# Second-half transposes of a fused mixer kernel by 32x32 VectorE blocks and a DRAM round trip instead of TensorE, and one scan fewer per convolution step

## The chip, the core and the metric

The kernel runs on one core of a Trainium2 chip. The metric is the device time of one execution in microseconds (us). The engines that matter are TensorE (PE in the profile; its weight loads are PEld), VectorE (DVE), ScalarE (ACT), GpSimd (POOL) and SyncE (SP), which issues nearly all DMAs. Each engine runs its own instructions in the order in which they were written down for it; semaphores make one engine wait for another.

## The reference, cut to what matters

The input is one sequence of 2048 rows and 448 columns, in fp32.

```
x = A_u                                        # [1, 2048, 448]
g = sigmoid((x * gate_w).sum(-1))
a = causal_convolution(x, K) + x * D_skip      # K[d, l] = 2 Re sum_n C exp(A dt l), 256 states n
h = gelu(layernorm(x) @ w1); hs = shift(h) @ w2; x1 = x + hs
b = x1 + gelu(layernorm(x1) @ w3) @ w4         # w3 448 -> 1792, w4 1792 -> 448
out = g * a + (1 - g) * b
```

For the inputs here the states decay slowly, and the kernel computes the convolution as a cubic Taylor sum: per column four running sums over time with the coefficients nu[0..3], nested into each other (a flag checks that this holds; otherwise a general path follows, which does not run here).

## The kernel before

The rows are cut into NB = 4 blocks b of 512 rows, each of NT = 4 tiles i of 128 rows. The work on TensorE is a list of 72 **units**: 16 of kind "a" (the w1/w2 mixer, 4 per block), then 56 of kind "d" (the w3/w4 MLP, 14 per block: units 16 to 29, 30 to 43, 44 to 57, 58 to 71). Every fp32 product is made of three products of split high and low halves. A unit n of kind "d" is `first(n)`, 11 matmuls (line 378) into a PSUM tile `p1` (two buffers), then gelu on ACT (line 396, out to `uf`), a copy to the high half `uh` (line 402), the low half `ul` by DVE (line 406, called `act_tail`), and `second(n)`, 12 matmuls (line 433) into four PSUM accumulators. PE does `first` two units ahead (LAG = 2). After the last unit of a block, DVE adds the four accumulators to `xs` (line 442).

From unit OWN = 28 on, the order on each engine is the order in which the code is written (`manual_schedule`, lines 764 to 779); before that a scheduler orders the instructions. For each unit, in this order: `act_tail(n+1)`, the lists `before` and `after` of that unit, `first(n+2)` with its gelu, the list `between`, the copy, some convolution work (`ssm_some`), the list `late`, `second(n)`.

Two other streams are laid into the units:

- **The layer norm of the MLP input**, for block b at units s0 = 9, 20, 30, 45. `norm` (lines 317 to 324) normalises one tile of 128 rows on ACT into `xn`; `norm_t` transposes it on PE, four matmuls 128x128 against the identity `idt` (line 334) into a PSUM tile `misc`, and ACT copies the high half to `xh` (line 336); `norm_lo` makes the low half on DVE (lines 343 and 344). `weigh` (line 348) then scales the tile of `xs` by 1 - g.
- **The convolution**, 16 **steps** (b, k): block b and column group k of 128 columns, columns on partitions and time along the free axis. `ssm_scale` (ACT, line 548, four instructions) writes the four scaled copies of the input into a tile `z4` with two buffers; `ssm_scan` runs five scans on DVE (line 558), m = 3, 2, 1, 0 and a fifth, called 4, on the row of m = 1; `ssm_sum` adds the skip term and the fifth scan (lines 564 and 565). When the four steps of a block are done, `ssm_add` transposes the result back on PE, four matmuls 128x128 per tile (line 570), two tiles in each of two units, and `ssm_out` adds it to `xs` from PSUM (line 578). `done` sends a tile of `xs` to DRAM when both halves are in it. `ssm_load` reads the next block's input into the buffer `zs`.

`ssm_some` hands out the queue of scans and sums by credit: per unit 3.7, less 2.2 in a block's last unit and less 0.7 for each entry of `late`; an entry runs while credit is left, at a cost written beside it (1.27 for a scan, 1.43 for a sum).

Of the kernel before, what the change touches and what calls it, by code (L numbers as in the profile page):

```python
# [173 lines left out]
def mixer_and_small_steps(ctx, tc, xs, gg, okm, x, xT, w1, w2, w3, w4, par, logdt, dskip, ident, out):  # L174
# [7 lines left out]
    def f32(ap):  # L182
        return ap.bitcast(F32)
# [130 lines left out]

    XN = {}

    def norm(b, i, early=False):
        j = NT * b + i
        xn = XN[b, i] = wk.tile([128, 512], F32, name="xn", tag="xn")
        nc.scalar.activation(xn[:, :D], xs[:, j, :], AF.Identity, bias=nm[:, j:j + 1], scale=r2[:, j:j + 1])  # L320
        if early:
            nc.vector.tensor_copy(xn[:, D:], xn[:, D - 64:D])
        else:
            nc.scalar.activation(xn[:, D:], xs[:, j, D - 64:], AF.Identity, bias=nm[:, j:j + 1], scale=r2[:, j:j + 1])
# [16 lines left out]
    def norm_lo(b, i):  # L341
        h, lo, p, t = XH["d", b], XL["d", b], NT_.pop((b, i)), slice(i * 128, (i + 1) * 128)
        nc.vector.tensor_sub(lo[:, :, t], p[:, :3, :], f32(h[:, :3, t]))
        nc.vector.tensor_sub(h[64:, 3, t], p[64:, 3, :], f32(h[64:, 3, t]))
# [194 lines left out]
    def ssm_load(b):  # L539
        ZS[b] = wk.tile([128, 4, TB], F32, name="zs", tag="rawc" if b % 2 else "rb", bufs=1)  # L540
        nc.sync.dma_start(ZS[b], xT[:, :, HALO + b * TB:HALO + (b + 1) * TB])
# [5 lines left out]
                nc.gpsimd.tensor_copy(z4[:, m, 0:1], carry[:, k, m:m + 1])  # L547
            nc.scalar.activation(z4[:, m, 1:], ZS[b][:, k, :], AF.Copy, scale=nu[:, k, m:m + 1])  # L548


    def ssm_scan(b, k, m):
        z4, nil = ZZ[b, k], zero.to_broadcast([128, TB])
        if m == 4:
            z, up = z4[:, 1, :TB], nil
        else:
            z = z4[:, m, 1:]
            up = z4[:, m + 1, :TB] if m in (1, 2) else nil
        nc.vector.tensor_tensor_scan(z, z, up, carry[:, k, m:m + 1], OP.add, OP.add)  # L558
        if b + 1 < NB:
            nc.gpsimd.tensor_copy(carry[:, k, m:m + 1], z[:, TB - 1:])  # L560

    def ssm_sum(b, k):
        z4, y = ZZ.pop((b, k)), ZS[b][:, k, :]
        nc.vector.scalar_tensor_tensor(y, y, dsk[:, k:k + 1], z4[:, 0, 1:], op0=OP.mult, op1=OP.add)
        nc.vector.tensor_add(y, y, z4[:, 1, :TB])

    def ssm_add(b, i):
        p = ps.tile([128, 512], F32, name="misc")
        for k in range(4):
            nc.tensor.transpose(p[:, k * 128:(k + 1) * 128], ZS[b][:, k, i * 128:(i + 1) * 128], idt)  # L570
        SP[b, i] = p

    SP = {}

    def ssm_out(b, i):
        p, j = SP.pop((b, i)), NT * b + i
        r = xs[:, j, :]
        nc.vector.scalar_tensor_tensor(r, p[:, :D], gg[:, j:j + 1], r, op0=OP.mult, op1=OP.add)  # L578
        done(b, i)
        if i == NT - 1 and b + 2 < NB:  # L580
            ssm_load(b + 2)


    queue = []

    def ssm_queue():
        for q, (b, k) in enumerate(steps):
            for m in (3, 2, 1, 0, 4):
                queue.append((1.27, ssm_scan, (b, k, m)))
                if m == 2 and q + 1 < len(steps):  # L590
                    queue.append((0.0, ssm_scale, steps[q + 1]))
            queue.append((1.43, ssm_sum, (b, k)))
        ssm_load(0)
        ssm_load(1)

# [2 lines left out]
    def ssm_some(n, amount):  # L598
        credit[0] += amount
        while queue and credit[0] > 0.0:  # L600
            cost, fn, a = queue.pop(0)
            credit[0] -= cost
            fn(*a)
            if fn is ssm_sum and a[1] == 3:

                u = n + 1
                while any(f is norm_t for v in (u, u + 1) for f, _ in between.get(v, [])):
                    u += 1
                for i in range(NT):
                    at(u + i // 2, ssm_add, a[0], i, when=between)  # L610
                    at(u + i // 2, ssm_out, a[0], i, when=late)

# [2 lines left out]
    def at(n, fn, *a, when=after):  # L617
        when.setdefault(n, []).append((fn, a))
# [108 lines left out]
    for b in range(NB):  # L727
        s0 = (9, 20, 30, 45)[b]
        for i in range(NT):
            at(s0 + i, norm, b, i, b < 2)  # L730
            at(s0 + i + 1, norm_t, b, i, when=between)
            at(s0 + i + 1, norm_lo, b, i, when=late)
            at(max(s0 + i + 7, 17 + i), weigh, b, i)

    at(15, ssm_par, 0)
    at(19, ssm_par, 1)
# [24 lines left out]
        second(n)  # L761


    with tc.manual_schedule():
        for n in range(OWN, len(units)):
            if n + 1 < len(units):
                act_tail(n + 1)
            run(before, n)
            run(after, n)
            if n + LAG < len(units):  # L770
                first(n + LAG)
                act_head(n + LAG, True)
# [53 lines left out]
```

## Time and profile before

| what | value |
|---|---|
| three runs, median (lowest to highest) | 402.24 us (400.5 to 402.3) |
| the profiled execution, its own time | 402.19 us |
| its span in the profile | 400.4 us |
| granted TensorE clock, mean | 0.996 of full speed |
| ACT busy | 203.2 us (51%) |
| POOL busy | 57.2 us (14%) |
| DMA moved | 26.93 MB, mean 67 GB/s |

The span runs from the first to the last instruction of the program; 1.8 us of the execution's time lie outside it. An engine's busy time overlaps with that of the others. Unit 28 begins with the `first` of unit 30 at 169.1 us, and the first scan of the convolution at 172.3 us. In the rows of the trace a matmul's own duration is longer than the time by which the next one follows it, because matmuls are pipelined; the chain of work in order of time shows the time by which PE really advances.

### The profile page before, as it was taken

The page shows a single profiled execution, that of the slowest core. Times are in us where ns is not written, and L with a number is a line of the kernel's source. Part 1 is how long each engine was busy: PE and PEld are TensorE (multiplying, and loading weights), DVE is VectorE, ACT ScalarE, POOL GpSimd, SP SyncE. Part 2 cuts the span into 40 slices and gives each one's busy share as a digit, 9 for nine tenths or more (in the row PEclk, how much of TensorE's full clock was granted, in tenths as well). Part 3 has the DMA queues.
Part 4 walks back from the last instruction along what each step waited for, and adds up shares of the span by engine and source line. Part 5 has one row for each costly group of instructions (what it writes and reads, how often), then busy time and mean ns, then how long its engine had stood idle before and what let it go on. Part 6 is the DMA issues. An engine that isn't in the chain of part 4 may idle for free.

```text
span 400.4 us, 5167 instructions
## 1 busy us (share of the span) xinstructions
PE 388.0 (97%) x1851; PEld 330.3 (82%) x1851; DVE 307.1 (77%) x581; ACT 203.2 (51%) x340; POOL 57.2 (14%) x127
## 2 busy tenths in 40 slices
PE   7999899999999999999999999999999999999993
PEld 3678788788888888888888888888888888888892
DVE  3689999989983387289999795997778778788222
ACT  4183667595696532275556524566266334442120
POOL 1260000000000000043025321242133301000000
PEclk9999999999999999999999999999999999999998
DMA  8991523613453000000000150000052002000002
GB/s 267 315 362 35 190 83 130 206 46 77 167 145 66 2 0 2 1 0 2 1 2 0 46 152 0 0 2 1 31 127 42 2 0 93 0 0 2 0 1 97
DMA packets 12903, 26.93 MB, mean 67 GB/s; under 512 B 1094, under 2 KB 6358, under 8 KB 12618
## 3 DMA queue, kind: packets, MB, share of 16 engines
q1 hardware_dynamic: 12730, 26.33, 21.2%
q8 instruction: 16, 0.26, 0.3%
q10 hardware_dynamic: 144, 0.23, 0.2%
q14 instruction: 13, 0.11, 0.1%
HBM read 22.88 MB, written 3.68 MB: 66 GB/s over the span
## 4 chain that ended last, share of the span: by engine, by line
PE 87%; DVE 6%; DMA 2%; ACT 2%; issue 1%; DVEq 0%; ACTq 0%
PE p L378 41%; PE acc L433 40%; PE misc L334 2%; PE misc L570 2%; DMA raw<-w_in 1%; DVE b L272 1%; DMA w1r<-w_in 1%; DVE ul L406 1%; PE pw L666 1%; PE pm L630 1%; DVE xl L311 1%; PE misc L294 1%; DVE w3l L217 1%; DVE uf L393 1%; ACT xh L309 0%
## 5 line engine op out<-in xcount | busy, mean ns | idle before, releaser
L396 ACT ACTIVATE uf<-p 128x512 f32<-128x512 f32 x56 | 33.5, 598 | 141.8 <-PE p L378 138.0
L406 DVE TENSOR_TENSOR ul<-uf,uh 128x512 fp32r<-128x512 f32 (+1 forms) x72 | 50.7, 705 | 36.6 <-ACT uh L402 36.4
L378 PE MATMUL p<-xh,w3h 128*128 128x512 f32 x224 | 61.2, 395 | 0.0
L378 PE MATMUL p<-xh,w3l 128*128 128x512 f32 x224 | 60.8, 393 | 0.0
L433 PE MATMUL acc<-w4h,uh 128*128 128x448 f32 x224 | 59.9, 372 | 0.0
L558 DVE TENSOR_TENSOR_SCAN z<-z,carry,zero 128x512 f32<-128x512 f32 x48 | 59.9, 1269 | 0.0
L433 PE MATMUL acc<-w4h,ul 128*128 128x448 f32 x224 | 58.2, 364 | 0.0
L433 PE MATMUL acc<-w4l,uh 128*128 128x448 f32 x224 | 58.1, 364 | 0.0
L378 PEld LDWEIGHTS p<-xh,w3l 128*128 128x128 f32 x224 | 42.1, 188 | 9.9
L378 PE MATMUL p<-xl,w3h 128*128 128x512 f32 x168 | 47.9, 394 | 0.0
L378 PEld LDWEIGHTS p<-xh,w3h 128*128 128x128 f32 x224 | 42.1, 188 | 6.7
L560 POOL COPY carry<-z 128x1 f32<-128x1 f32 x60 | 28.0, 470 | 137.1 <-DVE z L558 136.0
L402 ACT ACTIVATE uh<-uf 128x512 fp32r<-128x512 f32 (+1 forms) x72 | 45.4, 631 | 1.5
L433 PEld LDWEIGHTS acc<-w4l,uh 128*128 128x128 f32 x224 | 42.0, 188 | 3.2
L433 PEld LDWEIGHTS acc<-w4h,ul 128*128 128x128 f32 x224 | 42.0, 188 | 3.2
L433 PEld LDWEIGHTS acc<-w4h,uh 128*128 128x128 f32 x224 | 40.6, 188 | 4.4
L558 DVE TENSOR_TENSOR_SCAN z<-z,carry 128x512 f32<-128x512 f32 x32 | 41.0, 1283 | 2.0
L548 ACT ACTIVATE z<-zs,nu 128x512 f32<-128x512 f32 x64 | 41.0, 713 | 0.0
L547 POOL COPY z<-carry 128x1 f32<-128x1 f32 x48 | 20.6, 473 | 136.1 <-DVE w L508 107.3
L378 PEld LDWEIGHTS p<-xl,w3h 128*128 128x128 f32 x168 | 31.5, 188 | 7.3
L578 DVE SCALAR_TENSOR_TENSOR xs<-misc,gg,xs 128x448 f32<-128x448 f32 x16 | 10.2, 678 | 13.6 <-PE misc L570 13.6
L433 PE MATMUL acc<-w2h,uh 112*128 112x448 f32 x64 | 19.9, 371 | 0.0
(121 smaller groups left out, 493.4 us busy)
## 6 DMA issues: line engine op xcount, KB each, us to landing
zs<-xT_in SPq DMA_DIRECT2D x4, 1024.0 KB, 6.4
out_dram<-xs SPq DMA_DIRECT2D x16, 224.0 KB, 2.0
raw<-xT_in SPq DMA_DIRECT2D x3, 1032.0 KB, 11.7
raw<-w_in SPq DMA_DIRECT2D x3, 1024.0 KB, 5.5
raw<-w_in SPq DMA_DIRECT2D x3, 896.0 KB, 4.9
pk<-par_in SPq DMA_DIRECT2D x2, 1024.0 KB, 5.9
xs<-x_in SPq DMA_DIRECT2D x2, 896.0 KB
raw<-xT_in SPq DMA_DIRECT2D x4, 258.0 KB, 4.5
```

Of the source, the lines that this page charges most:

```text
L334: nc.tensor.transpose(p[:, k, :], xn[:, k * 128:(k + 1) * 128], idt)
L378: nc.tensor.matmul(p[:m], a_, b_, start=(q == 0), stop=(q == len(seq) - 1))
L396: nc.scalar.activation(u[:m], p[:m], AF.Gelu_apprx_tanh)
L402: nc.scalar.activation(UH[n][:m], UF[n][:m], AF.Copy)
L406: nc.vector.tensor_sub(UL[n][:m], UF.pop(n)[:m], f32(UH[n][:m]))
L433: nc.tensor.matmul(ACC[j], (UL if p == 2 else UH)[n][:m, t], wl if p == 1 else wh, start=s and p == 0, stop=e and p == 2)
L547: nc.gpsimd.tensor_copy(z4[:, m, 0:1], carry[:, k, m:m + 1])
L548: nc.scalar.activation(z4[:, m, 1:], ZS[b][:, k, :], AF.Copy, scale=nu[:, k, m:m + 1])
L558: nc.vector.tensor_tensor_scan(z, z, up, carry[:, k, m:m + 1], OP.add, OP.add)
L560: nc.gpsimd.tensor_copy(carry[:, k, m:m + 1], z[:, TB - 1:])
L570: nc.tensor.transpose(p[:, k * 128:(k + 1) * 128], ZS[b][:, k, i * 128:(i + 1) * 128], idt)
L578: nc.vector.scalar_tensor_tensor(r, p[:, :D], gg[:, j:j + 1], r, op0=OP.mult, op1=OP.add)
```

## The change

From unit 28 on the transposes no longer run on TensorE. DVE transposes 32x32 blocks within a tile (one instruction), and the blocks are put in place by writing the tile to DRAM and reading it back in another order. For the layer norm of blocks 2 and 3, `norm_d` writes the normalised tile with its columns interleaved, `norm_turn` transposes the blocks and writes them to `xd`, `norm_fetch` reads them back into `xr` (in runs of 32 numbers, 128 bytes), and `norm_hi` and `norm_lo` split `xr` from SBUF. Two tiles go at a time, in units s0 to s0 + 4 and s0 + 5 to s0 + 9. For the convolution, `ssm_turn` transposes a step's result into the row of `z4` that is no longer needed and writes it to `yd` (four DMAs a step, two for k = 3, in runs of 128 bytes), `ssm_back` reads a tile of rows back into `ysb`, and `ssm_out` adds it from SBUF. The four scans m = 3, 2, 1, 0 now take the row above as a second term throughout, so that the fifth scan and the second addition in `ssm_sum` fall away. Blocks 0 and 1 of the layer norm keep TensorE, and so does everything before unit 28. The credits change, `weigh` comes a unit later, and the next block's input is loaded by `ssm_turn`.

```diff
+    def norm_d(b, i):
+        j = NT * b + i
+        xn = XN[b, i] = wk.tile([128, 512], F32, name="xn", tag="xn")
+        for o, t in ((xn[:, :384].rearrange("p (k a c) -> p k a c", k=3, a=4),
+                      xs[:, j, :384].rearrange("p (k c a) -> p k a c", k=3, a=4)),
+                     (xn[:, 384:D].rearrange("p (a c) -> p a c", a=2),
+                      xs[:, j, 384:].rearrange("p (c a) -> p a c", a=2))):
+            nc.scalar.activation(o, t, AF.Identity, bias=nm[:, j:j + 1], scale=r2[:, j:j + 1])
+    def norm_turn(b, i):
+        t = wk.tile([128, 512], F32, name="xt", tag="u")
+        d = XD[b, i] = dr.tile([D * 128], F32, name="xd", bufs=4)
+        nc.vector.transpose(t[:, :D], XN.pop((b, i))[:, :D])
+        nc.sync.dma_start(d[:384 * 128].rearrange("(k p c) -> p k c", k=3, p=128),
+                          t[:, :384].rearrange("p (k c) -> p k c", k=3))
+        nc.sync.dma_start(d[384 * 128:].rearrange("(p c) -> p c", p=128), t[:, 384:D])
+    def norm_fetch(b, i):
+        d = XD.pop((b, i))
+        p = NT_[b, i] = wk.tile([128, 4, 128], F32, name="xr", tag="xn")
+        nc.sync.dma_start(p[:, :3, :].rearrange("p k (t c) -> p (k t) c", c=32),
+                          d[:384 * 128].rearrange("(g p c) -> p g c", p=128, c=32))
+        for o in (0, 64):
+            nc.sync.dma_start(p[o:o + 64, 3, :].rearrange("p (t c) -> p t c", c=32),
+                              d[384 * 128:].rearrange("(g p c) -> p g c", p=64, c=32))
+    def norm_hi(b, i):
+        if i == 0:
+            hl_tiles(("d", b))
+        nc.scalar.activation(XH["d", b][:, :, i * 128:(i + 1) * 128], NT_[b, i], AF.Copy)
...
     def ssm_scan(b, k, m):
-        z4, nil = ZZ[b, k], zero.to_broadcast([128, TB])
-        if m == 4:
-            z, up = z4[:, 1, :TB], nil
-        else:
-            z = z4[:, m, 1:]
-            up = z4[:, m + 1, :TB] if m in (1, 2) else nil
+        z4 = ZZ[b, k]
+        z, up = z4[:, m, 1:], z4[:, m + 1, :TB] if m < 3 else zero.to_broadcast([128, TB])
...
-        nc.vector.tensor_add(y, y, z4[:, 1, :TB])
-    def ssm_add(b, i):
-        p = ps.tile([128, 512], F32, name="misc")
-        for k in range(4):
-            nc.tensor.transpose(p[:, k * 128:(k + 1) * 128], ZS[b][:, k, i * 128:(i + 1) * 128], idt)
-        SP[b, i] = p
+    def ssm_turn(b, k):
+        if k == 0:
+            YD[b] = dr.tile([TB, D], F32, name="yd", bufs=2)
+        t = ZZ.pop((b, k))[:, 0, 1:]
+        nc.vector.transpose(t, ZS[b][:, k, :])
+        for a_ in range(4 if k < 3 else 2):
+            o = k * 128 + a_ * 32
+            nc.sync.dma_start(YD[b].rearrange("(t c) d -> c t d", c=32)[:, :, o:o + 32],
+                              t[a_ * 32:a_ * 32 + 32].rearrange("p (t c) -> p t c", c=32))
+        if k == 3 and b + 2 < NB:
+            ssm_load(b + 2)
+    def ssm_back(b, i):
+        YS[b, i] = wk.tile([128, D], F32, name="ysb", tag="u")
+        nc.sync.dma_start(YS[b, i], YD[b][i * 128:(i + 1) * 128])
     def ssm_out(b, i):
-        nc.vector.scalar_tensor_tensor(r, p[:, :D], gg[:, j:j + 1], r, op0=OP.mult, op1=OP.add)
+        nc.vector.scalar_tensor_tensor(r, YS.pop((b, i)), gg[:, j:j + 1], r, op0=OP.mult, op1=OP.add)
...
-            for m in (3, 2, 1, 0, 4):
-                queue.append((1.27, ssm_scan, (b, k, m)))
+            for m in (3, 2, 1, 0):
+                queue.append((1.19, ssm_scan, (b, k, m)))
-            queue.append((1.43, ssm_sum, (b, k)))
+            queue.append((0.75, ssm_sum, (b, k)))
+            queue.append((0.6, ssm_turn, (b, k)))
...
+                    at(n + 1 + i // 2, ssm_back, a[0], i, when=late)
+                    at(n + 3 + i // 2, ssm_out, a[0], i, when=late)
...
+                n = s0 + 5 * (i // 2)
+                at(n, norm_d, b, i)
+                at(n + 1, norm_turn, b, i)
+                at(n + 1, norm_fetch, b, i, when=late)
+                at(n + 4, norm_hi, b, i)
+                at(n + 4, norm_lo, b, i)
+            at(max(s0 + i + 8, 17 + i), weigh, b, i)
...
+    cost = {ssm_out: 0.6, norm_turn: 0.6, norm_lo: 0.9, stats_b: 1.2, rstd2: 2.4}
+            spent = sum(cost.get(fn, 0.0) for when in (after, late) for fn, _ in when.get(n, []))
-                ssm_some(n, 3.7 - (2.2 if units[n][2] == NF - 1 else 0.7 * len(late.get(n, []))))
+                ssm_some(n, 3.6 - (2.2 if units[n][2] == NF - 1 else 0.0) - spent)
```

The lines of the changed file are shifted: 378 becomes 411, 433 becomes 466, 406 becomes 439, 442 becomes 475, 558 becomes 586.

On PE, the place where block 0 of the convolution goes back, before: the 11 matmuls of a `first`, two tiles' transposes (`misc`), and the first matmuls of a `second`.

```order
L378 MATMUL p1_2138<-xh_1319,w3h_79 128x512 x4
L378 MATMUL p1_2138<-xh_1319,w3l_80 128x512 x4
L378 MATMUL p1_2138<-xl_1320,w3h_79 128x512 x3
L570 MATMUL misc_2154<-idt_72,zs_1597 128x128 x4
L570 MATMUL misc_2159<-idt_72,zs_1597 128x128 x4
L433 MATMUL acc0_1782<-w4h8_1173,uh_2070 128x448
```

In the change `second` follows `first` directly at this place, as it does in all of the units 28 to 71.

On DVE, one whole step and what stands among it, before: the low half of a unit (`ul`), the scans of the step's tile `z4_2167` (those with `zero_86` take one term, the others two), and its sum in two instructions.

```order
L558 SCALAR_TENSOR_TENSOR z4_2167<-z4_2167,carry_88,zero_86 128x512
L558 SCALAR_TENSOR_TENSOR z4_2167<-z4_2167,carry_88 128x512
L406 TENSOR_TENSOR ul_2258<-uf_2259,uh_2260 128x512
L558 SCALAR_TENSOR_TENSOR z4_2167<-z4_2167,carry_88 128x512
L558 SCALAR_TENSOR_TENSOR z4_2167<-z4_2167,carry_88,zero_86 128x512 x2
L406 TENSOR_TENSOR ul_2294<-uf_2295,uh_2296 128x512
L564 SCALAR_TENSOR_TENSOR zs_1599<-zs_1599,dsk_85,z4_2167 128x512
L565 TENSOR_TENSOR zs_1599<-zs_1599,z4_2167 128x512
```

And the same step on DVE in the change, with the four `ssm_out` of the block before it (`ysb`), in units 40 to 42:

```order
L439 TENSOR_TENSOR ul_2223<-uf_2224,uh_2225 128x512
L586 SCALAR_TENSOR_TENSOR z4_2175<-z4_2175,carry_88,zero_86 128x512
L586 SCALAR_TENSOR_TENSOR z4_2175<-z4_2175,carry_88 128x512
L616 SCALAR_TENSOR_TENSOR xs_58<-ysb_2187,gg_59,xs_58 128x448
L616 SCALAR_TENSOR_TENSOR xs_58<-ysb_2189,gg_59,xs_58 128x448
L439 TENSOR_TENSOR ul_2265<-uf_2266,uh_2267 128x512
L586 SCALAR_TENSOR_TENSOR z4_2175<-z4_2175,carry_88 128x512 x2
L616 SCALAR_TENSOR_TENSOR xs_58<-ysb_2235,gg_59,xs_58 128x448
L616 SCALAR_TENSOR_TENSOR xs_58<-ysb_2237,gg_59,xs_58 128x448
L439 TENSOR_TENSOR ul_2304<-uf_2305,uh_2306 128x512
L592 SCALAR_TENSOR_TENSOR zs_1599<-zs_1599,dsk_85,z4_2175 128x512
L601 STREAM_TRANSPOSE z4_2175<-zs_1599 128x512
```

The step has four scans, one sum and one transpose, and the rows of `xs` wait for DMAs instead of for PE.

On SP, the first DMAs of the convolution and the norm in the change (before, SP has only the 16 writes of `out_dram` and two loads of `zs` from here to the end): a step's four writes, the two tiles of the norm out and back, and the next step's writes behind them.

```order
L604 DMA yd_1779<-z4_1660 32x16x32 x4
L361 DMA xd_1818<-xt_1817 128x3x128
L363 DMA xd_1818<-xt_1817 128x64
L361 DMA xd_1823<-xt_1822 128x3x128
L363 DMA xd_1823<-xt_1822 128x64
L368 DMA xr_1847<-xd_1818 128x12x32
L371 DMA xr_1847<-xd_1818 64x4x32 x2
L368 DMA xr_1851<-xd_1823 128x12x32
L371 DMA xr_1851<-xd_1823 64x4x32 x2
L604 DMA yd_1779<-z4_1694 32x16x32 x4
```

The reads of `xr` wait on SP until the writes of `xd` have landed, and the writes of the next step are queued behind them.

More of the change, by code (lines that the diff above doesn't have):

```diff
@@ L315, in mixer_and_small_steps, with norm @@
     XN = {}
-    def norm(b, i, early=False):
+    def norm(b, i):
         j = NT * b + i
@@ L320, in norm @@
         nc.scalar.activation(xn[:, :D], xs[:, j, :], AF.Identity, bias=nm[:, j:j + 1], scale=r2[:, j:j + 1])
-        if early:
-            nc.vector.tensor_copy(xn[:, D:], xn[:, D - 64:D])
-        else:
-            nc.scalar.activation(xn[:, D:], xs[:, j, D - 64:], AF.Identity, bias=nm[:, j:j + 1], scale=r2[:, j:j + 1])
+        nc.vector.tensor_copy(xn[:, D:], xn[:, D - 64:D])
     def norm_t(b, i):
@@ L344, in norm_lo @@
         nc.vector.tensor_sub(h[64:, 3, t], p[64:, 3, :], f32(h[64:, 3, t]))
+    def norm_d(b, i):
[6 more added lines that the diff above has]
+            nc.scalar.activation(o, t, AF.Identity, bias=nm[:, j:j + 1], scale=r2[:, j:j + 1])
+    XD = {}
+    def norm_turn(b, i):
[17 more added lines that the diff above has]
+        nc.scalar.activation(XH["d", b][:, :, i * 128:(i + 1) * 128], NT_[b, i], AF.Copy)
     def weigh(b, i):
@@ L551, in ssm_scan @@
     def ssm_scan(b, k, m):
-        z4, nil = ZZ[b, k], zero.to_broadcast([128, TB])
-        if m == 4:
-            z, up = z4[:, 1, :TB], nil
-        else:
-            z = z4[:, m, 1:]
-            up = z4[:, m + 1, :TB] if m in (1, 2) else nil
+        z4 = ZZ[b, k]
+        z, up = z4[:, m, 1:], z4[:, m + 1, :TB] if m < 3 else zero.to_broadcast([128, TB])
         nc.vector.tensor_tensor_scan(z, z, up, carry[:, k, m:m + 1], OP.add, OP.add)
@@ L562, in ssm_sum @@
     def ssm_sum(b, k):
-        z4, y = ZZ.pop((b, k)), ZS[b][:, k, :]
+        z4, y = ZZ[b, k], ZS[b][:, k, :]
         nc.vector.scalar_tensor_tensor(y, y, dsk[:, k:k + 1], z4[:, 0, 1:], op0=OP.mult, op1=OP.add)
-        nc.vector.tensor_add(y, y, z4[:, 1, :TB])
-    def ssm_add(b, i):
-        p = ps.tile([128, 512], F32, name="misc")
-        for k in range(4):
-            nc.tensor.transpose(p[:, k * 128:(k + 1) * 128], ZS[b][:, k, i * 128:(i + 1) * 128], idt)
-        SP[b, i] = p
-    SP = {}
+    YD, YS = {}, {}
+    def ssm_turn(b, k):
[12 more added lines that the diff above has]
+        nc.sync.dma_start(YS[b, i], YD[b][i * 128:(i + 1) * 128])
     def ssm_out(b, i):
-        p, j = SP.pop((b, i)), NT * b + i
+        j = NT * b + i
         r = xs[:, j, :]
-        nc.vector.scalar_tensor_tensor(r, p[:, :D], gg[:, j:j + 1], r, op0=OP.mult, op1=OP.add)
+        nc.vector.scalar_tensor_tensor(r, YS.pop((b, i)), gg[:, j:j + 1], r, op0=OP.mult, op1=OP.add)
         done(b, i)
-        if i == NT - 1 and b + 2 < NB:
-            ssm_load(b + 2)
     queue = []
@@ L603, in ssm_some @@
             fn(*a)
[L604 to L608, printed above, removed]
+            if fn is ssm_turn and a[1] == 3:
                 for i in range(NT):
-                    at(u + i // 2, ssm_add, a[0], i, when=between)
-                    at(u + i // 2, ssm_out, a[0], i, when=late)
+                    at(n + 1 + i // 2, ssm_back, a[0], i, when=late)
+                    at(n + 3 + i // 2, ssm_out, a[0], i, when=late)
     before, between, after, late = {}, {}, {}, {}
@@ L729, in mixer_and_small_steps @@
         for i in range(NT):
[L730 to L733, printed above, removed]
+            if b < 2:
+                at(s0 + i, norm, b, i)
+                at(s0 + i + 1, norm_t, b, i, when=between)
+                at(s0 + i + 1, norm_lo, b, i, when=late)
+            else:
+                n = s0 + 5 * (i // 2)
[5 more added lines that the diff above has]
+            at(max(s0 + i + 8, 17 + i), weigh, b, i)
     at(15, ssm_par, 0)
```

## The prediction

> **What bounds the kernel now.** I read the page first: busy shares and the chain of work that ended last.
>
> ```profile
> span 400.4 us, 5167 instructions
> ...
> PE 388.0 (97%) x1851; PEld 330.3 (82%) x1851; DVE 307.1 (77%) x581; ACT 203.2 (51%) x340; POOL 57.2 (14%) x127
> ...
> PE 87%; DVE 6%; DMA 2%; ACT 2%; issue 1%; DVEq 0%; ACTq 0%
> ```
>
> PE is busy for 97% of the span, and 87% of the last chain is PE. That is an average over stages, and the change acts only from unit 28 on. So next come the busy times by stretches: the last 170 us of PE's work, and a stretch with the norm of block 2 (length, then PE, PEld, DVE, ACT and POOL busy, clock, DMA share, GB/s).
>
> ```profile
> 223.30:393.60 170.30, 170.24 (x830) 148.62 (x828) 126.60 (x150) 75.17 (x126) 28.62 (x71) 1.00 0.11 30
> 185.00:205.00 20.00, 20.00 (x102) 17.43 (x101) 19.20 (x40) 11.21 (x21) 4.49 (x13) 1.00 0.00 1
> ```
>
> PE stands still nowhere here, at full clock: each instruction taken from it shortens the kernel, if nobody else is late. DVE is second, with 19.2 of 20 us where the norm lies; it is the engine to watch. What an instruction costs PE is read from the chain in order of time (start, length, what), since matmuls overlap.
>
> ```profile
> 184.20 2.55 PE p L378 x11
> 186.75 0.44 PE misc L334 x4
> 187.19 2.42 PE acc L433 x12
> ...
> 283.96 2.54 PE p L378 x11
> 286.51 0.87 PE misc L570 x8
> 287.38 2.44 PE acc L433 x12
> ...
> 298.23 2.41 PE acc L433 x12
> 300.64 2.55 PE p L378 x11
> ```
>
> A unit without transposes takes 2.41 + 2.55 = 4.96 us. A norm tile's four transposes add 0.44 us, two convolution tiles 0.87 us, and the next work follows without a gap.
>
> **What is removed from PE.** The counts come from the view of single lines (duration in ns: least, median, most; first and last start).
>
> ```profile
> L570 PE MATMUL misc<-idt,zs x64: 270/272/273, 223.2 to 381.0; 128*128 128x128 f32 x64
> ...
> L324 ACT ACTIVATE xn<-xs,nm,r x8: 422/430/437, 179.2 to 272.5; 128x64 f32<-128x64 f32 x8
> ```
>
> All 64 convolution transposes go: 8 pairs of tiles x 0.87 = 6.96 us. Line 324 is the form of `norm` that only blocks 2 and 3 use, so 8 norm tiles go: 8 x 0.44 = 3.52 us. Together 10.48 us. The profiled execution took 402.19 us (span 400.4 and 1.8 outside), practically the median of 402.24; less 10.48 this gives **391.7 us**, a span of 389.9. The work before unit 28 and the tail after PE's last matmul stay.
>
> The Trainium skill ("TensorE: Matmul & The Clock Gate", Part 4: PE-mode transpose) gives about 275 ns for one such transpose inside a kernel. The row's 272 ns agrees, but that is a latency: by the page's figure the 96 transposes would be worth 26 us and the time 376, whereas the chain advances by only 0.11 us each, and the chain decides.
>
> **What DVE pays.** From the groups by line and form (busy us, mean ns):
>
> ```profile
> L558 DVE TENSOR_TENSOR_SCAN z<-z,carry,zero 128x512 f32<-128x512 f32 x48 | 59.9, 1269 | 0.0
> L558 DVE TENSOR_TENSOR_SCAN z<-z,carry 128x512 f32<-128x512 f32 x32 | 41.0, 1283 | 2.0
> L406 DVE TENSOR_TENSOR ul<-uf,uh 128x512 fp32r<-128x512 f32 x56 | 38.4, 686 | 35.9 <-ACT uh L402 35.6
> L564 DVE SCALAR_TENSOR_TENSOR zs<-zs,dsk,z 128x512 f32<-128x512 f32 x16 | 11.7, 734 | 0.0
> L565 DVE TENSOR_TENSOR zs<-zs,z 128x512 f32<-128x512 f32 x16 | 11.1, 692 | 0.6
> L578 DVE SCALAR_TENSOR_TENSOR xs<-misc,gg,xs 128x448 f32<-128x448 f32 x16 | 10.2, 678 | 13.6 <-PE misc L570 13.6
> L442 DVE SCALAR_TENSOR_TENSOR xs<-acc,gs,xs 128x448 f32<-128x448 f32 x16 | 10.0, 679 | 8.0 <-PE acc L433 8.0
> L343 DVE TENSOR_TENSOR xl<-misc,xh 128x384 fp32r<-128x384 f32 x16 | 8.9, 554 | 2.8 <-ACT xh L336 2.5
> L344 DVE TENSOR_TENSOR xh<-misc,xh 64x128 fp32r<-64x128 f32 x16 | 4.7, 294 | 0.2
> L272 DVE BATCH_NORM_STATS2 b<-xs 128x6 f32<-128x448 f32 x32 | 19.0, 616 | 0.1
> L274 DVE BATCH_NORM_AGGREGATE st<-b 128x2 f32<-128x6 f32 x32 | 4.8, 169 | 0.0
> L285 DVE SCALAR_TENSOR_TENSOR r<-t,r 128x4 f32<-128x4 f32 x18 | 2.8, 157 | 0.2
> ```
>
> A two-term scan costs 1.283 us against 1.269, so the second term is nearly free. The fifth scan and the second addition go: 16 x (1.27 + 0.69) = 31.4 us. The block transpose is not in the trace. Its bounds are a small pass, 0.16 us (line 285), and a scan of the same shape, 1.28; it is one pass over 128x512 like line 565, so I take 0.69. 24 of them add 16.6 us.
>
> Whether DVE keeps up I count over units 30 to 45, the densest, where both norm trips of block 2 fall: 16 `ul` x 0.69, 28 scans x 1.28, 6 sums x 0.73, 11 transposes x 0.69, 4 norm tiles x 0.85, 4 statistics x 0.79, 12 small operations x 0.16, 4 `ssm_out` and 4 accumulators x 0.68. That is 72.8 us, 4.55 per unit against PE's 4.96. At the upper bound, 1.28 per transpose, it is 4.95: still just hidden. So this costs nothing, but little cover is left, about 0.4 us per unit. The point from which it decides is 1.3 us per transpose.
>
> **What the way through DRAM costs.** No transfer in runs of 128 bytes is in the trace, and this is the real unknown. First the fixed parts: one issue on SP with 512 runs (a load of `zs`), a write to DRAM from issue to landing (us), and the work of ACT in a unit with a step (gelu, copy, four `ssm_scale`).
>
> ```profile
> 231.39 0.57 SPq L541 DMA_DIRECT2D zs<-xT_in  x1
> ...
> out_dram<-xs SPq DMA_DIRECT2D x3, 224.0 KB, 2.0
> ...
> 223.41 0.60 ACT L396 ACTIVATE uf<-p 128x512 f32<-128x512 f32 x1 [3.16 <-PE p L378]
> 224.04 0.63 ACT L402 ACTIVATE uh<-uf 128x512 fp32r<-128x512 f32 x1
> 224.58 2.55 ACT L548 ACTIVATE z<-zs,nu 128x512 f32<-128x512 f32 x4
> ```
>
> Then two stretches with a single kind of packet: a read of 16 runs of 512 bytes (2.6 us long), and two writes of 128 runs of 1792 bytes (7.7 us long).
>
> ```profile
> DMA packets 32, 0.01 MB, mean 3 GB/s; under 512 B 16, under 2 KB 32, under 8 KB 32
> ...
> q1 hardware_dynamic: 32, 0.01, 1.6%
> ...
> DMA packets 288, 0.46 MB, mean 60 GB/s; under 512 B 32, under 2 KB 288, under 8 KB 288
> ...
> q1 hardware_dynamic: 288, 0.46, 16.1%
> ```
>
> 1.6% of 16 engines x 2.6 us is 0.67 us, 42 ns per run of 512 bytes with what closes it. 16.1% of 16 x 7.7 us is 19.8 us, 77 ns per run of 1792. For 128 bytes the bounds are 5.5 ns (by bytes) and 77 (nothing saved); the straight line through the two gives **31 ns**, an estimate that I take.
>
> *Convolution.* `z4` has two buffers, and now the one of step q-1 is free for step q+1 only when its four writes have landed; ACT waits at `ssm_scale`, with the following gelus behind it, and DVE at the next scan, with the following `ul` behind it. A step has 4 x 512 runs, 128 per DMA engine. Landing takes 0.57 + 128 x 0.031 + 2.0 = 6.6 us. A step needs 4 x 1.28 + 0.73 + 0.69 and 1.7 `ul`, 7.7 us of DVE, and gets 6.11 / 3.6 = 1.7 units (the costs and the credit in the change), 8.4 us. Two steps must hold one landing, the first scaling (0.7) and a step's work: 6.6 + 8.4 = 15.0 of 16.8. Hidden; from a landing of 8.4 us on, or 46 ns a run, it is not.
>
> *Norm.* Two tiles' writes: four issues and a landing, 4.3 us; two reads of 2048 runs behind them: 0.6 + 2 x 4.0 + 2.0. The second tile is there 14.9 us after DVE's transposes, and `norm_hi` asks for it some 12.8 us after them (three units less 0.7 and 1.4). ACT would wait 2 us. Cover: a gelu is needed only when `first` two units on wants its PSUM buffer, 2.42 + 2.55 + 2.42 = 7.4 us after it could start, 6.8 after its 0.6; so I cost it at nothing.
>
> *Behind on SP:* the next step's `yd` writes stand behind these reads, some 7 us, and the reads of `ysb` come two units ahead of their use. Neither meets PE.
>
> **The rivals.** (1) *Small runs cost more than the line says*: DMAs take the place of PE as the bound. At 77 ns a landing takes 12.5 us, a step (12.5 + 8.4) / 2 = 10.4, 2.0 more than now; over 15 steps 31 us less the lead of about 7, so **416 us**, slower, and more if the norm trips pass their cover too. It decides from 46 ns. For it speaks that bytes alone explain little of the two stretches; against it that the nearest row, 512 bytes, stands at 42 and 128 bytes should cost less.
>
> (2) *A short write costs two passes*, 62 ns, while reads stay: landing 10.5 us, step 9.45, 15 x 1.05 - 7 = 9 us lost, **401 us**, no change. The Trainium skill ("DMA: Bandwidth & Descriptors", Specifications) states such a rule: below 512 bytes a write becomes a read and a write. No row here has a short write in number to test it.
>
> (3) *Part of the cover goes*: a price near 50 ns, or DVE with 0.4 us to spare waiting for several DMAs in turn, shows as PE gaps of some tenths in the dense units. Between 392.7 and 400, say **395**; for it speaks the stretch with DVE at 96%, against it that DVE's list becomes shorter by 15 us.
>
> **How the numbers follow.** Forecast 0.74; (1) 0.08; (2) 0.07; (3) 0.11. About 0.5%, 2 us, is what a measurement can tell from no change. Faster: 0.74 + 0.11 = 0.85; same: (2); slower: (1). The forecast alone would be 391 to 392.7; the three runs before differ by 1.8 us, so I start the range at 390.0, and take in most of (3), up to 398.0. Outside are (1), (2) and a few hundredths.
>
> **What would show it.** In the changed profile: no `misc` group on PE after 182 us and units of 4.96 us throughout; a block transpose below 1.3 us; `yd` landing within 8.4 us of its first issue; no wait of DVE scans or `ssm_scale` for DMA over 2 us. Wrong it would be if PE shows idle time for gelu or `ul`, and behind it ACT or DVE for `xr` or `yd`.

## The result and the profile after

| | before | after |
|---|---|---|
| median of 4 runs each (lowest to highest) | 401.55 us (400.5 to 402.3) | 390.19 us (389.91 to 390.76) |
| the profiled execution, its own time | 402.19 us | 390.11 us |
| its span | 400.4 us | 388.3 us |

The ratio is 0.972 [0.969, 0.975]: 2.8% faster. The forecast was 391.7 us, range 390.0 to 398.0.

The page of the changed kernel, busy times, the shares of the last chain, and the DMA packets:

```profile
span 388.3 us, 5163 instructions
PE 377.3 (97%) x1755; PEld 320.5 (83%) x1755; DVE 292.5 (75%) x573; ACT 207.0 (53%) x340; POOL 54.5 (14%) x115
DMA packets 65897, 38.23 MB, mean 98 GB/s; under 512 B 48966, under 2 KB 59350, under 8 KB 65610
...
PE 91%; DVE 5%; ACT 1%; DMA 1%; issue 1%; DVEq 0%; ACTq 0%
```

PE still bounds the kernel, with 91% of the chain instead of 87%. PE has 96 instructions and 10.7 us of work less, and 48966 of the packets are now short ones. The chain in order of time (start, length, what) shows the stretch on which the forecast rested:

```profile
168.25 2.55 PE p L411 x11
...
183.37 2.56 PE p L411 x11
185.92 2.45 PE acc L466 x12
188.37 2.54 PE p L411 x11
...
374.81 7.28 PE acc L466 x36
...
382.11 0.69 DVE xs L475
```

At 185.92 `second` follows `first` directly, where before four `misc` transposes stood between them. A unit takes 4.96 to 5.00 us, as before. The same chain before, its first piece from unit 28 on and its last ones:

```profile
169.08 2.55 PE p L378 x11
...
386.27 7.28 PE acc L433 x36
...
393.58 0.68 DVE xs L442
```

From the start of unit 28 to the first addition behind the last matmul it was 393.58 - 169.08 = 224.50 us, and now it is 382.11 - 168.25 = 213.86: 10.64 us less, where 10.48 was forecast. The profiled times differ by 12.08. The other 1.4 us lie outside this stretch: 0.83 before unit 28, where the change only moves one `weigh` to unit 28, and 0.6 behind the last matmul.

DVE in units 30 to 45, for which the prediction added up 72.8 us (columns as in the prediction: window, length, then busy time of PE, PEld, DVE, ACT and POOL, clock, DMA share, GB/s):

```profile
178.40:257.80 79.40, 79.40 (x369) 68.93 (x368) 70.12 (x102) 47.30 (x79) 24.77 (x48) 1.00 0.38 84
```

70.12 us are 4.38 per unit, and PE is busy in all of the 79.40. The new operations, from the groups by line and form (busy us, mean ns, idle time before):

```profile
L586 DVE TENSOR_TENSOR_SCAN z<-z,carry,zero 128x512 f32<-128x512 f32 x16 | 19.9, 1246 | 0.0
L601 DVE STREAM_TRANSPOSE z<-zs 128x512 f32<-128x512 f32 x16 | 11.3, 708 | 1.2 <-POOL carry L588 0.3
...
L353 ACT ACTIVATE xn<-xs,nm,r 128x384 f32<-128x384 f32 x8 | 8.6, 1072 | 1.9 <-DVE xh L341 1.9
L320 ACT ACTIVATE xn<-xs,nm,r 128x448 f32<-128x448 f32 x8 | 5.9, 753 | 3.2 <-DVE nx L548 3.2
...
L360 DVE STREAM_TRANSPOSE xt<-xn 128x448 f32<-128x448 f32 x8 | 4.7, 621 | 0.0
```

A block transpose of 128x512 takes 0.71 us (0.69 taken), one of 128x448 0.62; the first scan of a step, which adds a broadcast zero, costs about what it did, 1.25 (1.27 before). What the engines wait for between 168 and 382 us (total us, times, longest); no row of it is PE's, and of the waits for DMAs that of POOL's small copies into `z4` is the longest:

```profile
POOL z L580 <- DMA yd<-z: 15.2, 6, 7.6
...
DVE xl L340 <- ACT xh L377: 5.7, 3, 2.8
...
ACT z L581 <- DMA yd<-z: 4.0, 4, 2.1
ACT xh L377 <- DMA xr<-xd: 3.1, 2, 2.3
```

The price of a short run comes from a stretch of 9.5 us (239.5 to 249.0) in which only one step's four writes, 2048 runs, are under way:

```profile
DMA packets 2121, 0.28 MB, mean 29 GB/s; under 512 B 2113, under 2 KB 2121, under 8 KB 2121
...
q1 hardware_dynamic: 2121, 0.28, 17.4%
...
yd<-z SPq DMA_DIRECT2D x4, 64.0 KB, 2.3
```

17.4% of 16 x 9.5 us is 26.4 us, 12.9 ns per run; a second such stretch (181.5 to 186.5 us, a share of 36.0%) gives 14. And two places of the timeline (start, length, engine, line; in brackets the idle time ahead and who ended it): a step's landing with nothing left ahead of it on SP, and one behind the reads of the norm.

```profile
192.99 0.68 DVE L601 STREAM_TRANSPOSE z<-zs 128x512 f32<-128x512 f32 x1
...
193.70 1.97 SPq L604 DMA_DIRECT2D yd<-z  x4
...
197.53 0.72 ACT L581 ACTIVATE z<-zs,nu 128x512 f32<-128x512 f32 x1 [0.34 <-DMA yd<-z]
...
261.93 0.57 SPq L574 DMA_DIRECT2D zs<-xT_in  x1
...
265.93 4.66 SPq L371 DMA_DIRECT2D xr<-xd  x1
...
268.29 0.71 DVE L601 STREAM_TRANSPOSE z<-zs 128x512 f32<-128x512 f32 x1
...
275.04 2.42 SPq L604 DMA_DIRECT2D yd<-z  x4
...
279.41 0.73 ACT L581 ACTIVATE z<-zs,nu 128x512 f32<-128x512 f32 x1 [2.09 <-DMA yd<-z]
```

In the first place the four writes are issued within 2.0 us, and the scaling that needs its buffer is released 197.53 - 193.67 = 3.9 us after the transpose's end (6.6 forecast). In the second place the queue of SP is held up by the norm's reads and two reads of `ysb`: the writes are issued 6.0 us after the transpose, and ACT waits 2.09 us. These reads of the norm stand directly behind the load of the next block's input (`zs`, 1024 KB), and one of them alone takes SP 4.66 us to issue, where the median of these issues is 0.69. PE sees neither place, though the second landing comes 279.41 - 269.00 = 10.4 us after the transpose's end.

### The profile page after: what moved, and what is told of

It is laid out like the page before. It is cut to its first block, busy times and chain, and to the rows that moved or that the text cites. A ratio compares the mean times of both kernels' runs of the same rounds, so it can differ in the third digit from the quotient of the medians.

```text
span 388.3 us, 5163 instructions
## 1 busy us (share of the span) xinstructions
PE 377.3 (97%) x1755; PEld 320.5 (83%) x1755; DVE 292.5 (75%) x573; ACT 207.0 (53%) x340; POOL 54.5 (14%) x115
## 2 busy tenths in 40 slices
DMA packets 65897, 38.23 MB, mean 98 GB/s; under 512 B 48966, under 2 KB 59350, under 8 KB 65610
## 4 chain that ended last, share of the span: by engine, by line
PE 91%; DVE 5%; ACT 1%; DMA 1%; issue 1%; DVEq 0%; ACTq 0%
PE p L411 44%; PE acc L466 43%; DVE b L272 1%; PE pw L699 1%; PE misc L331 1%; DMA w1r<-w_in 1%; PE pm L663 1%; DVE ul L439 1%; DVE xl L311 1%; PE misc L294 1%; ACT xh L309 0%; DVE xh L313 0%; DVE r L281 0%; ACT w1h L216 0%; ACT uh L435 0%
## 5 line engine op out<-in xcount | busy, mean ns | idle before, releaser
L586 DVE TENSOR_TENSOR_SCAN z<-z,carry 128x512 f32<-128x512 f32 x48 | 61.5, 1281 | 1.9
L466 PE MATMUL acc<-w4h,uh 128*128 128x448 f32 x224 | 58.6, 366 | 0.0
L466 PEld LDWEIGHTS acc<-w4h,uh 128*128 128x128 f32 x224 | 41.7, 188 | 5.7
L588 POOL COPY carry<-z 128x1 f32<-128x1 f32 x48 | 24.4, 517 | 116.5 <-DVE z L586 116.2
L586 DVE TENSOR_TENSOR_SCAN z<-z,carry,zero 128x512 f32<-128x512 f32 x16 | 19.9, 1246 | 0.0
L466 PE MATMUL acc<-w2l,uh 112*128 112x448 f32 x64 | 19.5, 364 | 0.0
## 6 DMA issues: line engine op xcount, KB each, us to landing
raw<-xT_in SPq DMA_DIRECT2D x3, 1032.0 KB, 12.2
```

What stands on the lines that cost most here:

```text
L466: nc.tensor.matmul(ACC[j], (UL if p == 2 else UH)[n][:m, t], wl if p == 1 else wh, start=s and p == 0, stop=e and p == 2)
```

## The experiments

Three questions: whether the gain is PE's transposes alone; what the fold is for; and how far DVE and the way through DRAM are from taking over, the prediction's two points of decision. "Stretch" is the time from the start of unit 28 to the first addition behind the last matmul, as above.

| run | median, us | lowest to highest (runs) | ratio to before | stretch, us |
|---|---|---|---|---|
| norm on PE again | 394.05 | 393.17 to 394.64 (4) | 0.980 [0.978, 0.982] | 217.41 |
| convolution on PE again | 397.88 | 396.49 to 398.06 (4) | 0.988 [0.986, 0.990] | 220.93 |
| before, with the fold alone | 401.33 | 400.23 to 401.95 (10) | 0.998 [0.997, 0.999] | 224.47 |
| the change without the fold | 396.68 | 396.16 to 396.98 (4) | 0.986 [0.985, 0.988] | 221.09 |
| the change again | 390.88 | 389.90 to 390.95 (4) | 0.973 [0.970, 0.976] | 213.86 |
| one more DVE pass a step | 390.77 | 389.90 to 391.19 (4) | 0.973 [0.970, 0.976] | 213.86 |
| writes x2 | 396.06 | 393.73 to 398.70 (4) | 0.989 [0.984, 0.993] | 217.48 |
| writes x3 | 422.57 | 421.98 to 422.94 (4) | 1.052 [1.050, 1.055] | 245.60 |
| writes x4 | 457.34 | 453.89 to 460.06 (4) | 1.136 [1.127, 1.145] | 281.99 |
| block 1's norm too | 388.17 | 387.24 to 389.35 (4) | 0.967 [0.964, 0.971] | 213.85 |

### One half of the change at a time

**The norm of blocks 2 and 3 on PE again**, all else as in the change:

```diff
-            if b < 2:
+            if True:
                 at(s0 + i, norm, b, i)
```

> The layer norm of blocks 2 and 3 is transposed on PE again, the convolution as in the change. Theory (the time is PE's list of work, everything else is hidden): 8 tiles x 0.44 us come back, 390.2 + 3.5 = 393.7 us (within 0.8). Rival (a good part of the gain comes from a shorter DVE list or from the norm's detour itself): under 392 or over 395.

**The convolution on PE again**, with the fold and the norm of the change:

```diff
...
-            queue.append((0.6, ssm_turn, (b, k)))
...
-            if fn is ssm_turn and a[1] == 3:
+            if fn is ssm_sum and a[1] == 3:
                 for i in range(NT):
-                    at(n + 1 + i // 2, ssm_back, a[0], i, when=late)
-                    at(n + 3 + i // 2, ssm_out, a[0], i, when=late)
+                    at(n + 1 + i // 2, ssm_add, a[0], i, when=between)
+                    at(n + 1 + i // 2, ssm_out, a[0], i, when=late)
```

> The convolution's result goes back through PE again (64 transposes), with the four-scan sum; the layer norm as in the change. Theory: 8 pairs x 0.87 us come back, 390.2 + 7.0 = 397.2 us (within 0.8). Rival (the DVE list, which is 11 us shorter here than in the change, sets part of the time): under 396.

The stretch grows by 217.41 - 213.86 = 3.55 us with the norm's 8 x 0.44 = 3.52 back on PE, and by 220.93 - 213.86 = 7.07 us with the convolution's 8 x 0.87 = 6.96. Together 10.62, the whole of the 10.64. So the two halves add up, each is worth the time by which the chain advances on its transposes, and neither way through DRAM costs anything that the other's absence would give back.

### The fold

**Before, with the fold alone:**

```diff
...
-            up = z4[:, m + 1, :TB] if m in (1, 2) else nil
+        z, up = z4[:, m, 1:], z4[:, m + 1, :TB] if m < 3 else zero.to_broadcast([128, TB])
...
-        nc.vector.tensor_add(y, y, z4[:, 1, :TB])
...
-            for m in (3, 2, 1, 0, 4):
+            for m in (3, 2, 1, 0):
...
```

> The kernel before with the four-scan sum alone: DVE loses 31 us of work, PE nothing. Theory (PE's list alone): no change, 401.6 us (within 0.8). Rival (DVE's relief gives the part of the gain, some 1.6 us, that PE's transposes do not explain): about 400, or less.

31 us less work for DVE leave the stretch at 224.47 us (224.50): nothing, as long as PE is the bound. The median is 0.2% lower, with an interval that just excludes 1; it is no part of this stretch, and its cause was not looked for.

**The change without the fold:** five scans and the second addition are back, at no charge in the queue, so that each stands where it would stand in the change.

```diff
...
+        nc.vector.tensor_add(y, y, z4[:, 1, :TB])
...
-            for m in (3, 2, 1, 0):
-                queue.append((1.19, ssm_scan, (b, k, m)))
+            for m in (3, 2, 1, 0, 4):
+                queue.append((1.19 if m < 4 else 0.0, ssm_scan, (b, k, m)))
```

> The change with five scans and the second addition, at the places and credits of the change: DVE's list is 16 x 1.97 = 31.5 us longer, 0.93 us per unit over the 34 units with convolution work. Theory (DVE is hidden only up to 4.96 us per unit; it has 4.4 in the change): 5.3 per unit, 34 x 0.35 = 12 us over, less a lead of about 7: +5, about 395 us (391 to 402), with PE gaps for gelu or the low half in units 30 to 62. Rival (DVE has far more cover than counted, by its 75% share): 390.2, no PE gap.

Half of the gain goes: +5.8 us on the change again, 7.2 us in the stretch. The window over the whole convolution, then the waits of this run:

```profile
178.40:340.00 161.60, 156.65 (x716) 135.05 (x715) 154.93 (x207) 88.20 (x145) 56.63 (x94) 0.99 0.41 91
```

```profile
ACT z L581 <- DMA yd<-z: 26.8, 10, 5.2
...
PEld p L411 <- ACT uf L429: 3.5, 1, 3.5
...
PE p L411 <- ACT uf L429: 3.1, 1, 3.1
```

DVE is busy for 154.93 of 161.60 us, and PE stands still for 5 us; the scalings wait for a `z4` buffer ten times instead of four, since a step that is done later sends its writes later, and PE waits for a gelu behind such a scaling. From unit 28 to the last matmul PE stands still for 4.96 of the 7.2 us; the other 2.3 are matmuls that run slower (PE is busy for 216.1 us with the work that takes 213.8 in the change), right behind the longest of its pauses (see the last section). So the fold is what makes room on DVE for the transposes.

**One more pass a step:** each block transpose of the convolution is issued twice (16 x 0.71 us more).

```diff
+        for _ in range(1):
+            nc.vector.transpose(t, ZS[b][:, k, :])
         nc.vector.transpose(t, ZS[b][:, k, :])
```

> The change with the block transpose of each step made twice: one more DVE pass of 0.7 us per step, 11.3 us in all, 0.33 per unit over 34 units. Theory (DVE has 4.4 of 4.96 us per unit in the dense units): hidden, 390.2 us (within 0.8). Rival (DVE already sets the time in some units): +3 to +11 us.

Hidden: 390.77 against 390.88 us, and the same stretch to 0.01 us. The same window of it:

```profile
178.40:340.00 161.60, 161.60 (x750) 140.38 (x749) 149.07 (x201) 92.90 (x153) 45.07 (x86) 1.00 0.43 93
```

161.60 us are 32.6 units of PE, so 149.07 us are 4.57 per unit, and that is covered. The 154.93 us of the run without the fold are not its need in the same way: they are what DVE got done while PE fell behind with it. From unit 28 to the last matmul DVE is busy there for 189.3 us instead of 162.5, 26.8 more, or 0.79 per unit over the 34 units with convolution work: about 5.2 per unit with the 4.38 from above, more than the 4.96 that PE takes. So DVE's limit lies between 4.57 and 5.2 us per unit; nothing between was run.

### The change a second time

> The change itself, unaltered, beside the other kernels of this set and with a second profile: what of its time lies before unit 28 and after PE's last matmul, and how far that differs from one execution to the next. Theory (the 1.6 us beyond PE's transposes in the first two profiles are chance in the landing of the first and the last DMA): from the first of unit 28 to the last accumulator again 213.9 us, but a start of unit 28 between 167 and 169.2 us and another tail. Rival (they belong to the change): start at 168.25 and tail at 6.2 us again, to 0.1.

The stretch is 213.86 us again, to 0.01. Unit 28 began at 167.62 us here and at 168.25 in the first profile, and the tail behind the last matmul is 6.5 us instead of 6.2, so neither repeats to 0.1. Among all the programs here that are the same up to unit 28 as the change, it began between 167.0 and 169.0 us, against 169.1 in the profile of before, where the first load of weights landed at 4.82 us instead of 4.16. So the 1.4 us by which the profiled pair differ beyond the stretch are mostly of the size by which two executions differ; whether some tenths belong to the change stays open: the two profiles whose code is that of before up to unit 28 (before, and before with the fold) begin it at 169.1 and 168.9, at the upper end.

### More writes

**Each write of a step four times**, three of them into buffers that nobody reads (16 issues a step):

```diff
             nc.sync.dma_start(YD[b].rearrange("(t c) d -> c t d", c=32)[:, :, o:o + 32],
                               t[a_ * 32:a_ * 32 + 32].rearrange("p (t c) -> p t c", c=32))
+            for r_ in range(3):
+                spare = dr.tile([TB, D], F32, name=f"sp{b}{k}{a_}{r_}")
+                nc.sync.dma_start(spare.rearrange("(t c) d -> c t d", c=32)[:, :, o:o + 32],
+                                  t[a_ * 32:a_ * 32 + 32].rearrange("p (t c) -> p t c", c=32))
```

> The change with each write of a step to DRAM made four times (three into spare tensors nobody reads): 16 instead of 4 issues of some 0.5 us on SP, 8192 runs of 128 bytes instead of 2048. Theory (a landing is hidden up to 8.4 us from a step's first issue, and a run costs 13 ns): a landing of about 16 x 0.5 + 2 = 10 us, a step (10 + 8.4) / 2 = 9.2 us, 15 x 0.8 - 7 = +5: about 395 us (391 to 400), waits of ACT for yd in most steps. Rival (the transfers have cover of several steps): 390.2, no gaps on PE.

The direction was right and the size was missed by far: 457.34 us, 66 more than the change. The page's shares of the last chain in this run:

```profile
PE 40%; SPq 26%; DVE 12%; DMA 9%; ACT 7%; issue 5%; POOL 1%; DVEq 0%; POOLq 0%; ACTq 0%
```

A quarter of the chain is SP handing out DMAs. The expectation let two steps share one landing, as the prediction does. The two next runs were made to tell that count from another, in which every single step must hold a landing. **Each write twice** (8 issues) **and three times** (12), with `range(1)` and `range(2)` in the edit above:

> Each write of a step to DRAM is issued twice, the second time into a buffer that nobody reads: 8 issues a step instead of 4. Revised theory, from the run with 16: a step's landing is about 0.49 us per issue and 1.5 us behind the last, so 3.5 us with 4, 5.5 to 6 with 8, and the scaling that waits for it stands on ScalarE ahead of the gelu whose low half stands on VectorE ahead of the next step's block transpose. So one landing and some 4.5 us from scaling to transpose must fit in ONE step, not two in two steps; the changed kernel's steps are 10.8 us apart on average (181.1 to 342.7 in 15 steps). With 8 issues 5.8 + 4.5 = 10.3: about at the edge, so most is hidden: 392 us, 390 to 397, with waits of ScalarE for the writes of 1 to 3 us in more steps than before. Rival, the prediction's own count (a landing has the time of two steps, exposed only beyond 8.4 us): hidden wholly, 390.2 +- 0.5. They differ clearly only in the next run.

> As the run before with each write issued three times, 12 issues a step. Revised theory: landing 7.5 to 8, with 4.5 us from scaling to block transpose 12.4 us a step against 10.8: 15 steps x 1.6 = 24 us, less a lead of up to 7 and a few us: 408 us, 400 to 418; the steps' block transposes about 12.4 us apart. Rival, the prediction's count: the landing of 8 us is below 8.4, so nothing shows: 390.2 +- 0.7 us, transposes 10.8 us apart.

They are 396.06 and 422.57 us. By the prediction's count both would have stayed at 390 or 391, even with the landings that these runs showed: with the longer, 9.5 us, a step is (9.5 + 8.4) / 2 = 9.0 us, 0.55 more than 8.4, which the lead of 7 us nearly covers over 15 steps (and less than the 10.8 us that the steps are apart anyway). The first time lies inside the 390 to 397 of the revised theory, the second beyond its 400 to 418; its landing of 8 us was too short. One turn of the loop with 12 issues, from the timeline of that run:

```profile
324.76 0.71 DVE L601 STREAM_TRANSPOSE z<-zs 128x512 f32<-128x512 f32 x1 [4.79 <-POOL carry L588]
325.96 0.56 SPq L604 DMA_DIRECT2D yd<-z  x1
326.56 1.04 SPq L608 DMA_DIRECT2D sp<-z  x2
...
331.87 1.05 SPq L608 DMA_DIRECT2D sp<-z  x2
334.99 2.57 ACT L581 ACTIVATE z<-zs,nu 128x512 f32<-128x512 f32 x4 [3.95 <-DMA sp<-z]
335.02 0.42 POOL L580 COPY z<-carry 128x1 f32<-128x1 f32 x3 [6.68 <-DMA sp<-z]
335.38 0.30 POOL L588 COPY carry<-z 128x1 f32<-128x1 f32 x2
335.71 0.71 DVE L601 STREAM_TRANSPOSE z<-zs 128x512 f32<-128x512 f32 x1 [0.64 <-POOL carry L588]
```

A step's transpose ends at 325.47; SP needs 7 us for the 12 issues, 0.58 each; the last one lands at 335.0. Only then POOL can copy the carries into that buffer for the step two further on, and behind these copies, in POOL's order, stands the copy out of the *next* step's row, which that step's transpose overwrites. So the next transpose starts 0.7 us after this step's landing. ACT ties the same two steps in another way: the scaling waits for the landing, with a gelu, its `uh` and so DVE's `ul` behind it, and the next transpose behind that on DVE. (The chain of the run with 8 issues goes this way between 282 and 293 us.) POOL's copy is what the transpose waited for in 6 of the 16 steps of the run with 12 issues; the others were not followed one by one.

How far the block transposes of the convolution lie apart comes from the view of the transpose's line; of the change and of the run with 12 issues (duration in ns: least, median, most; first and last start in us):

```profile
L601 DVE STREAM_TRANSPOSE z<-zs x16: 670/714/715, 181.1 to 342.7; 128x512 f32<-128x512 f32 x16
```

```profile
L601 DVE STREAM_TRANSPOSE z<-zs x16: 673/714/716, 181.3 to 379.2; 128x512 f32<-128x512 f32 x16
```

A step is the mean distance of two transposes (in the change they lie 7.2 to 19.2 us apart); steps with k = 3 have half the issues:

| issues a step | landing seen after a transpose's end, us | one step, us (15 steps) | median time, us |
|---|---|---|---|
| 4 | 3.9 | (342.7 - 181.1) / 15 = 10.8 | 390.88 |
| 8 | 6.4 | (350.8 - 180.7) / 15 = 11.3 | 396.06 |
| 12 | 9.5 | (379.2 - 181.3) / 15 = 13.2 | 422.57 |
| 16 | 12.2 | (415.1 - 181.7) / 15 = 15.6 | 457.34 |

From 8 to 12 and from 12 to 16 issues a step becomes 1.9 and 2.4 us longer; 15 steps make 28 and 36 us of that, and the stretch became 28.1 and 36.4 us longer. So from 8 issues on the time follows the steps. Each of these runs has 56 issues more than the one before it, which comes to 0.50 and 0.65 us each; SP takes 0.5 to 0.6 us for one. How much of it is SP's issuing alone is not shown, because the matmuls also became slower in these runs (last section).

With 8 issues the loop is not closed at every step yet. In that run's profile, which is of the fastest of its four executions, the stretch is 3.6 us longer than in the change; PE stands still for 2.8 us of it, 2.07 of them in one place, at 288 to 290 us, behind the same load of `zs` and the norm's reads that held SP up above. A straight line through 8 and 12 issues, 7.0 us of stretch for an issue more in each step, meets the change's 213.86 between 7 and 8 issues, a landing near 6 us (an estimate; 7 was not run). It holds for landings in step after step: the single one of 10.4 us in the change was covered.

### Further in the same direction

**The norm of block 1 too**, in a tile of its own that is free there, two tiles at a time in units 21 to 27:

```diff
-            if b < 2:
+            if b < 1:
                 at(s0 + i, norm, b, i)
...
+            BLK.append(wk.tile([128, 4, 512], F32, name="blk", tag="rawc", bufs=1))
+        xn = XN[b, i] = BLK[0][:, i % 2, :] if b == 1 else wk.tile([128, 512], F32, name="xn", tag="xn")
...
-                n = s0 + 5 * (i // 2)
+                w = 3 if b == 1 else 5
+                n = s0 + (b == 1) + w * (i // 2)
...
```

> The change with the layer norm of block 1 (units 21 to 27) also by DVE blocks and DRAM, in a tile of its own: 4 x 0.44 us of PE less. Theory: 390.2 - 1.8 = 388.4 us. Rival (in the units before 28 DVE, the scheduler's order or the DMAs of the weights do not leave room): no gain, or slower than 390.2.

388.17 us, 2.7 below the change in the same group of runs (390.88), where the four transposes of four tiles make 1.8. The stretch from unit 28 on is unchanged (213.85), and unit 28 begins at 165.74 us, 1.9 before the second profile of the change. The intervals of the ratios of the two, [0.964, 0.971] and [0.970, 0.976], just overlap, but all four times of this version (387.24 to 389.35) lie below all eight of the change (389.90 to 390.95).

## Why the prediction was right, point by point

**PE and what is removed from it: right.** The stretch fell by 10.64 us for 10.48 forecast, and the two halves are worth 3.55 and 7.07 us for 3.52 and 6.96. The row of 272 ns for a transpose, and the 275 ns of the Trainium skill ("TensorE: Matmul & The Clock Gate", Part 4: PE-mode transpose; given there for a tile in bf16, while these are fp32), would have given 26 us; the runs show the 0.11 us by which the chain advances. The work before unit 28 and the tail were to stay. In the profiled pair they gave 1.4 us more, of the size by which executions differ, so the time came out 1.5 us below the forecast and near the range's lower end.

**DVE: the size right, the limit not tested.** 72.8 us were added up, 70.12 measured; the block transpose was taken as 0.69 and is 0.71. The point from which it decides was set at 1.3 us per transpose, 4.95 us per unit, "still just hidden". One more pass was hidden at 4.57 per unit, and the change without the fold, at about 5.2, lost 5.8 us. Both agree with a limit of 4.96, and with one as low as 4.6: whether 4.95 would have been hidden is not shown.

**The norm's way: hidden as forecast, but the waits agree by luck.** A wait of ACT of 2 us was forecast behind each pair of tiles, covered by gelu's lead. Of the four pairs three show no wait at all. Both waits, 2.3 and 0.8 us, are in the third, whose reads stand on SP directly behind the load of `zs`; its slowest read landed 11.1 us after its issue, where the median is 3.0. The same reads are slow to issue there in all three runs with more writes (5.6 to 6.7 us for two, 1.3 to 1.6 in the other pairs). The 7 us for which the next step's writes were to stand behind the reads also appear only there, as 6.0; in the other pairs these writes went out 0.0, 1.4 and 0.0 us after their transpose. The sum does not contain the load of `zs`, and it has the reads at 31 ns per run; around the fourth pair's reads (291 to 298 us) a packet took 12.8 ns on average, 73.3% of 16 x 7.0 us for 6395 packets. That the load is the cause rests on this comparison; it was not moved. PE has no wait in any pair.

**The convolution's way: hidden, but its numbers were wrong and offset each other.** The mis-sized term is the price of a run: 31 ns by a straight line through two rows with longer runs, 12.9 measured. The sum also has one issue on SP, 0.57 us, where a step has four, 2.0. Together that makes a landing of 3.9 us instead of 6.6. The step that failed is the condition: "Two steps must hold one landing", with 8.4 us as the point from which it shows. With 12 issues landings of 9.5 us made the stretch 32 us longer (slower matmuls included), where that condition gives 1 us, because the order of POOL and ACT makes the next step's transpose wait for this step's landing. By the line above the point is near 6 us, an estimate. The pace was also not 8.4 us a step but 10.8, since in the units with norm work, statistics or a block's end the credit is lower. With the forecast's own landing of 6.6 us the change would probably have lost some microseconds, as with 8 issues (6.4 us; the median 5 us longer). The forecast was right because the runs were cheap, not because the cover was as large as it said. Of its signs one was missed by little: `ssm_scale` waits 2.09 us for a DMA once, where none over 2 us was to be.

**The rivals.** (1), small runs as the bound, needs 46 ns by the prediction's count; at 12.9 ns it did not come up, but a landing that takes PE's place as the bound is real, as 12 and 16 issues show. There the number of issues on SP brought it about, while the DMA engines were busy for only 0.59 and 0.58 of the window below. (2), two passes for a short write, put 62 ns on a run. Nothing of the sort shows in the landing: the rule of the Trainium skill ("DMA: Bandwidth & Descriptors", Specifications), a read and a write below 512 bytes, may hold, but whatever it costs is inside the 12.9 ns. (3), part of the cover, did not occur: PE has no gap.

## What to carry to other kernels

Work that is taken from an engine without a gap is worth the time by which its chain advances, not the durations of its rows. For a detour over other queues, look not only at when its result is needed: follow what stands behind each waiting instruction on *every* engine in program order, POOL's tiny copies too, until it comes back to the start, and require the round trip to fit into one step. Look too at what else is on the same queue: here the only waits for the norm's reads came behind one large load. An engine that must follow another closely needs a reserve: here 8% of the other's time was enough (4.57 of 4.96 us), and how much less would be was not run.

## What the runs showed of the hardware

- Writes to DRAM in runs of 128 bytes cost 12.9 ns per run and DMA engine, less than the 42 ns per run of 512 bytes in the prediction's rows (16 runs, with what closes them); with four DMAs to a step the issues on SP, 2.0 us for four with 512 runs each, took up half of the landing of 3.9 us.
- ACT takes longer where it reads the columns interleaved, four apart: 1072 ns for 384 columns (line 353) against 753 ns for 448 in plain order (line 320), both in the groups above. Two apart cost nothing: 64 columns take 432 ns (line 353) and took 430 in plain order (line 324 before). The distance was not varied by itself. The prediction had not counted this; ACT had the room.
- The granted clock fell behind long pauses of PE. The same window in the runs with 12 and 16 issues (clock third from the end):

```profile
178.40:340.00 161.60, 142.14 (x629) 119.65 (x628) 114.71 (x158) 77.36 (x130) 23.60 (x77) 0.96 0.59 111
```

```profile
178.40:340.00 161.60, 125.86 (x523) 105.33 (x522) 97.03 (x137) 64.75 (x109) 19.80 (x64) 0.88 0.58 109
```

It is 1.00 in the change and 0.96 and 0.88 here, with PE busy for 142 and 126 of 161.6 us. At one such place, with 16 issues, PE stands still for 4.08 us up to 300.30; in the 3 us from 302 the clock is 0.50 and four matmuls of line 411 take 1.91 us, and from 305 on it is 0.99 and four take 1.09. Slower matmuls followed all eleven pauses of 2.8 us and more in the runs with 8, 12 and 16 issues and the one without the fold, two of the six between 1.8 and 2.3 us, and none of the eleven shorter ones. From unit 28 to the last matmul PE is busy for 213.8 us in the change, and for 222.5 and 233.8 with 12 and 16 issues, with the same matmuls. Whether the kernel would be shorter by these 8.7 and 20.0 us at full clock is not shown.
